# Batch 1's convolution on 64-by-32 tiles in a causal-convolution and low-rank-mixer kernel, with two-group slots up to group 9 and batches 3 to 7 loaded and convolved a slot later

## Chip, cores, metric

One core of one Trainium2 chip. The metric is the device time of one execution in microseconds (us); with one core it is that core's time. The kernel before takes 325.07 us (median; 324.9 to 325.2). Within a trace the span is a little shorter (323.2 us for a run of 324.98 us), and all instants below are microseconds from the start of the span.

## The reference, cut to what matters

```python
# x: (8, 4224, 192); weight: (8 heads, 7 taps); U: (4224, 32); V: (32, 4224); w_ch1: (192, 768); w_ch2: (768, 192)
w = softmax(weight, axis=-1)
# causal convolution along the sequence, one set of 7 taps per head of 24 channels
y = einsum('hk,bskhg->bshg', w, windows_of_7(x_padded)).reshape(B, S, D)
# mixer: a low-rank product along the sequence, then two products along the channels
h = (y.transpose(0, 2, 1) @ U) @ V
u = y + h.transpose(0, 2, 1)
out = u + relu(u @ w_ch1) @ w_ch2
```

## The kernel before

TensorE does everything that is a product. The 264 tiles of 128 sequence rows make 33 groups of 8; each batch is 33 tiles, so a batch ends inside a group. A group goes through these helpers, whose names stand in the schedule (line numbers in profiles are those of the kernel before; those of the changed kernel are 6 higher from the convolution on):

- `conv32` (L339) or `conv` (L369): a batch's convolution as products with band matrices. `conv32` works on eight 64-by-32 tiles of the array, but needs `xb_sb`, a copy of x shifted by whole blocks and half blocks. `conv` works on four 64-by-64 tiles straight from `x_sb`. Evictions from PSUM go to `y_sb`.
- `t` and `s` (L402, L428): the product with U, for a whole batch. `h` (L457) is the product with V, and VectorE adds it to y into `u_sb` (L479).
- `transp` (L498): SyncE transposes `u_sb` by DMA into `uT`.
- `w1` (L554): 36 matmuls of the first product from `uT`, with 12 relu evictions; `w2` (L583): 12 matmuls of the second product for two tiles, plus an addition on VectorE and the output DMA on SyncE.

The shifted copy is made by GpSimd in six steps; its buffer is single:

```python
xbs = ctx.enter_context(tc.tile_pool(name="xbs", bufs=1))
...
def x_shift(b):
    xbt[b] = xbs.tile([P, NB1, D], BF16, name="xb_sb")
    ...                       # same(): L293 and L295, ahead(): L305, all nc.gpsimd.tensor_copy
    return [same(0, m), same(m, NB0, (NB0, NB1)),
            ahead(0, 0, m), ahead(0, m, NB0), ahead(1, 0, m), ahead(1, m, NB1)]
```

The same GpSimd queue issues the loads of x (four per batch), each held back until a named first or second product has run (`x_load(b, q, after)`). The order of everything is written out in slots: first the first products of some groups, then second products in pieces of two tiles, and other work hung on piece numbers (`c2:0:3` is three heads of batch 2's convolution from head 0 on, with letters for the evicting engines, A for ScalarE and D for VectorE; `d1` is batch 1's convolution by `conv`; `l2:2` a load of batch 2; `x3:4` four steps of batch 3's shifted copy; `h8` the residual of group 8 followed by its transpose; in the change, `X` is GpSimd's part of batch 1's copy and `w0:0` one of SyncE's transfers for it):

```python
SLOTS = [
    ([0], [], {}),
    ([1], [0], {0: ["h0"], 1: ["h3", "l2:2"], 2: ["l2:3"]}),
    ([2], [1], {0: ["d1", "h1"], 1: ["t1"], 3: ["s1"], 4: ["h4", "x2:6"]}),
    ([3], [2], {1: ["h5"], 3: ["h6"]}),
    ([4, 5], [3, 4, 5], {0: ["h7"], 2: ["c2:0:3:AAD"], 3: ["c2:3:3:AAD"],
        4: ["c2:6:2:A", "x3:4"], 6: ["t2"], 8: ["s2"], 9: ["h8"], 11: ["h9"]}),
]
nh = 10                       # next group to get its h and its transpose
for k in range(5, 14):        # slots [6, 7, 8], [9, 10, 11], ... [30, 31, 32]
    ...                       # h of groups nh, nh+1, nh+2 at pieces 5, 8 and 11
LOADS = {2: [(1, 5), (1, 5)], 3: [(4, 1), (4, 4), (5, 1), (5, 4)]}
for b in range(4, B):         # batch b's loads wait for first products of groups 3b-6 and 3b-5
    g = 3 * b - 6
    LOADS[b] = [(g, 0), (g, 3), (g + 1, 0), (g + 1, 3)]
```

The transpose of group 12 is issued in the last pieces of the slot of groups 6 to 8, and group 12 is wanted only after the whole slot of groups 9 to 11.

## Time and profile before

| | kernel before |
|---|---|
| time, us | 325.07 |
| span of the profiled run, us | 323.2 |
| TensorE busy | 317.6 us, 98% |
| granted TensorE clock | 0.9 or more in all 40 slices, mean 1.00 |
| median landing of a quarter of x, of a transpose | 6.9 us, 3.5 us |
| `h` and transpose ahead of the slot that uses them | one group more than needed |

The chain of waits in order of time, for the slot of groups 9 to 11: three groups' first products, then the first part of a convolution.

```profile
109.46 11.76 PE ps L554 x108
121.22 0.47 PE ps L339 x11
```

The view of the tile `uT`, SyncE's transposes alone, first all of them and then those issued between 130 and 140 us (counts, durations of the issue in ns, then the time from issue to landing, the arrival of the last data, in us):

```profile
L498 SPq DMA_TRANSPOSE uT<-u_sb x31: 1274/1437/2920, 27.1 to 291.6; - x31
DMA to landing us min/median/max: 3.2/3.5/8.3
```
```profile
L498 SPq DMA_TRANSPOSE uT<-u_sb x3: 1274/1537/2271, 132.0 to 139.0; - x3
DMA to landing us min/median/max: 4.2/4.9/7.9
```

The reader should not stop at the median. As long as loads of x go on, one transpose in each slot takes about twice as long: the one issued at 67.3 us took 8.3 us to land, those at 110.7, 139.0 and 167.6 us took 6.7, 7.9 and 7.1. Each of the last three is issued within 1 us of a load of x (GpSimd issues them at 111.0, 138.5 and 166.7). In the kernel before this costs nothing, because the group is not wanted for another whole slot (issued at 139.0, wanted at 165.57).

### The profile page before, as it was taken

How to read it: one execution, taken by the hardware profiler on the slowest of the kernel's cores; microseconds unless marked ns; L12 is line 12 of the kernel's file. 1: busy time of each engine (PE TensorE's matmuls, PEld its weight loads, DVE VectorE, ACT ScalarE, POOL GpSimd, SP SyncE). 2: the span in 40 equal slices, each digit the busy share in tenths (PEclk: the TensorE clock that was granted, in tenths of full speed). 3: DMA queues.
4: the chain of work that ended last, by engine and by line, in shares of the span. 5: the costliest groups of instructions: out<-in, count | busy, mean ns of one | idle time of the engine just before them, and what ended most of it. 6: DMA issues, size and time to landing. Idle time of an engine off the chain costs nothing.

```text
span 323.2 us, 9583 instructions
## 1 busy us (share of the span) xinstructions
PE 317.6 (98%) x3996; PEld 223.7 (69%) x3996; DVE 268.6 (83%) x551; ACT 170.0 (53%) x344; POOL 142.7 (44%) x111
## 2 busy tenths in 40 slices
PE   8999999999999999999999999999999999999995
PEld 3747676478677647866864884687797497487495
DVE  6769989987977986997898699789888897896863
ACT  1766724860874397088239609824903902912910
POOL 8764179728957983992897497000000000000000
PEclk9999999999999999999999999999999999999999
DMA  9999993999998999599499957138268059048035
GB/s 106 192 191 183 206 209 100 196 192 257 208 135 200 246 142 190 166 189 209 130 237 192 181 149 194 52 105 231 61 178 262 3 150 275 18 121 271 2 121 173
DMA packets 122906, 53.51 MB, mean 166 GB/s; under 512 B 87760, under 2 KB 122832, under 8 KB 122864
## 3 DMA queue, kind: packets, MB, share of 16 engines
q1 hardware_dynamic: 84528, 38.08, 45.4%
q0 software_dynamic: 38192, 14.73, 39.2%
q8 instruction: 31, 0.51, 0.7%
q10 hardware_dynamic: 144, 0.10, 0.1%
q14 instruction: 11, 0.09, 0.1%
HBM read 29.49 MB, written 25.95 MB: 172 GB/s over the span
## 4 chain that ended last, share of the span: by engine, by line
PE 92%; ACT 3%; DMA 2%; DVE 1%; issue 0%; POOL 0%; POOLq 0%
PE ps L583 42%; PE ps L554 39%; PE ps L339 3%; PE ps L457 3%; DMA x_sb<-in_x_dram 2%; PE ps L402 2%; ACT rl_sb L568 2%; PE ps L369 1%; ACT y_sb L256 1%; PE ps L509 1%; DVE u_sb L479 1%; DVE rl_sb L570 1%; PE ps L524 0%; PE ps L428 0%; POOL x_sb L79 0%
## 5 line engine op out<-in xcount | busy, mean ns | idle before, releaser
L568 ACT ACTIVATE rl_sb<-ps 128x512 bf16<-128x512 f32 x233 | 124.3, 604 | 108.0 <-PE ps L554 96.0
L583 PE MATMUL ps<-W_sb,rl_sb 128*128 128x192 bf16 x1584 | 141.2, 246 | 0.2
L583 PEld LDWEIGHTS <-rl_sb 128*128 128x128 bf16 x1584 | 128.3, 98 | 11.8 <-issue 11.5
L554 PE MATMUL ps<-uT,W_sb 64*128 64x512 bf16 x1188 | 131.7, 376 | 0.0
L570 DVE TENSOR_SCALAR rl_sb<-ps 128x512 bf16<-128x512 f32 x163 | 105.3, 688 | 15.7 <-PE ps L554 15.4
L554 PEld LDWEIGHTS <-W_sb 64*128 64x128 bf16 x1188 | 66.9, 94 | 60.4 <-issue 3.9
L592 DVE TENSOR_TENSOR out_sb<-ps,u_sb 128x384 f32<-128x384 f32 (+1 forms) x133 | 70.4, 551 | 25.5 <-PE ps L583 25.0
L305 POOL COPY xb_sb<-x_sb 32x3072 bf16<-32x3072 bf16 (+1 forms) x24 | 67.4, 2824 | 0.5
L479 DVE TENSOR_TENSOR u_sb<-y_sb,ps 128x192 bf16<-128x192 bf16 (+1 forms) x168 | 66.3, 461 | 0.0
L293 POOL COPY xb_sb<-x_sb 128x3072 bf16<-128x3072 bf16 x12 | 32.7, 2742 | 42.1 <-PE ps L339 32.2
L256 ACT ACTIVATE y_sb<-ps 128x384 bf16<-128x384 f32 (+4 forms) x90 | 38.3, 520 | 9.7 <-PE ps L339 7.4
L79 POOL DMA_DIRECT2D x_sb<-in_x_dram x32 | 27.0, 848 | 9.6 <-PE ps L457 3.8
L258 DVE CAST y_sb<-ps 128x408 bf16<-128x408 f32 (+4 forms) x36 | 19.1, 578 | 1.3 <-PE ps L369 1.0
L457 PE MATMUL ps<-tt_sb,V_sb 32*128 32x192 bf16 x264 | 12.4, 246 | 0.1
L339 PE MATMUL ps<-x_sb,band 64*32 64x384 bf16 x192 | 12.1, 333 | 0.0
L339 PE MATMUL ps<-xb_sb,band 64*32 64x384 bf16 x192 | 12.1, 332 | 0.0
L457 PEld LDWEIGHTS <-V_sb 32*128 32x128 bf16 x264 | 4.7, 92 | 7.3 <-issue 7.3
L416 ACT ACTIVATE tt_hi<-ps 128x192 bf16<-128x192 f32 x8 | 2.6, 330 | 11.9 <-PE ps L402 11.9
L369 PE MATMUL ps<-x_sb,band 64*64 64x240 bf16 (+3 forms) x192 | 8.0, 276 | 0.2 <-DMA x_sb<-in_x_dram 0.2
L339 PEld LDWEIGHTS <-band 64*32 64x32 bf16 x384 | 4.5, 89 | 5.2 <-issue 2.4
L153 PE MATMUL ps<-zz 128*128 128x512 f32 (+1 forms) x10 | 6.7, 816 | 1.1 <-DVE zz L143 1.1
L369 PEld LDWEIGHTS <-band 64*64 64x64 bf16 x192 | 6.0, 106 | 2.1 <-issue 1.4
(65 smaller groups left out, 71.3 us busy)
## 6 DMA issues: line engine op xcount, KB each, us to landing
out_dram<-out_sb SPq DMA_DIRECT2D x131, 192.0 KB, 2.7
x_sb<-in_x_dram POOLq DMA_DIRECT2D x14, 384.0 KB, 6.9
x_sb<-in_x_dram POOLq DMA_DIRECT2D x7, 432.0 KB, 6.7
x_sb<-in_x_dram POOLq DMA_DIRECT2D x7, 408.0 KB, 8.0
x_sb<-in_x_dram POOLq DMA_DIRECT2D x1, 504.0 KB, 7.3
uT<-u_sb SPq DMA_TRANSPOSE x31, 3.5
x_sb<-in_x_dram POOLq DMA_DIRECT2D x1, 480.0 KB, 5.6
W_sb<-in_moe_w_ch_dram POOLq DMA_DIRECT2D x2, 192.0 KB, 7.8
```

The costliest lines, as they stand in the source:

```text
L79: return nc.gpsimd.dma_start(out=xt[b][HB * r : HB * r + HB, s0:s1, :], in_=x[b, blk * HB : (blk + s1 - s0) * HB, :].rearrange("(j p) d -> ...
L256: nc.scalar.activation(out=out, in_=in_, func=ACT.Copy)
L293: nc.gpsimd.tensor_copy(out=xbt[b][:, s0:s1, :], in_=xt[b][:, s0 + 1 : s1 + 1, :])
L305: nc.gpsimd.tensor_copy(out=xbt[b][q, s0:s1, :], in_=xt[b][q, s0:s1, :])
L339: nc.tensor.matmul(out=pp[r][QB * cg : QB * cg + QB, 0 : nk[r] * GS], lhsT=w[hr], rhs=t[hr, st : st + 2 * nk[r] - 1 : 2, hs], start=True, ...
L457: nc.tensor.matmul(out=banks[pr][:, a * D : (a + 1) * D], lhsT=V_sb[32 * q : 32 * q + 32, (j // 8) * 2 + j % 2, :], rhs=ttb[b][32 * q : 32 ...
L479: nc.vector.tensor_tensor(out=u_group(g)[:, i : i + n, :, hf, :], in0=yt[b][:, run[0] : run[0] + n, :].rearrange("p n (c k) -> p n c k", c=3),
L554: last = nc.tensor.matmul(out=pps[m][hf][:], lhsT=W1_sb[HB * hf : HB * hf + HB, c, m * P : (m + 1) * P], rhs=uTt[g][HB * hf : HB * hf + HB ...
L568: nc.scalar.activation(out=rl[:, m, hf, :], in_=pp[hf][:], func=ACT.Relu)
L570: nc.vector.tensor_scalar_max(out=rl[:, m, hf, :], in0=pp[hf][:], scalar1=0.0)
L583: last = nc.tensor.matmul(out=cps[:, a * D : (a + 1) * D], lhsT=rlt[g][:, m, hf, (i + a) * P : (i + a + 1) * P], rhs=W2_sb[:, m, :], start ...
L592: nc.vector.tensor_tensor(out=o[:, 0:n, :].rearrange("p n (c k) -> p n c k", c=3), in0=cps[:, 0 : n * D].rearrange("p (n c k) -> p n c k", ...
```

## The change

Its intent: batch 1's convolution costs 3.24 us on 64-by-64 tiles and its evictions hold the end for 5.6 us. The change puts it on 64-by-32 tiles in three pieces between second products. The shifted copy it needs is made half by GpSimd (three steps) and half by three SyncE transfers. To make room, the early slots take two groups instead of one or three, the loads, copies and convolutions of batches 3 to 7 come a slot later, and `h` is made one group less far ahead; below, this distance is called the lookahead.

```diff
+    def x_ahead(b, r, n):
+        ...
+        nc.sync.dma_start(out=xbt[b][q, s0:s1, :], in_=xt[b][q, s0:s1, :])
     SLOTS = [
-        ([0], [], {}),
-        ([1], [0], {0: ["h0"], 1: ["h3", "l2:2"], 2: ["l2:3"]}),
-        ([2], [1], {0: ["d1", "h1"], 1: ["t1"], 3: ["s1"], 4: ["h4", "x2:6"]}),
-        ([3], [2], {1: ["h5"], 3: ["h6"]}),
-        ([4, 5], [3, 4, 5], { ... "c2" at 2, 3, 4, "x3:4" at 4, "t2" at 6, "s2" at 8, "h8" at 9, "h9" at 11 }),
+        ([0], [], {0: ["X", "w0:0", "w1:0"]}),
+        ([1], [0], {0: ["h0"], 1: ["h3"], 2: ["w0:1"]}),
+        ([2], [1], {0: ["h1"], 2: ["c1:0:3:AAD"], 3: ["c1:3:3:AAD"], 4: ["c1:6:2:AD", "x2:6"]}),
+        ([3], [2, 3], {0: ["t1"], 1: ["s1"], 2: ["h4"], 5: ["h5"]}),
+        ([4, 5], [4, 5], {0: ["h6"], 3: ["h7"], 5: ["c2:0:2:A"], 6: ["c2:2:3:AAD"], 7: ["c2:5:3:AAD"]}),
+        ([6, 7], [6, 7], {0: ["x3:4", "t2"], 1: ["s2"], 2: ["h8"], 5: ["h9"]}),
+        ([8, 9], [8, 9], {0: ["h10"], 2: ["c3:0:2:A"], 3: ["c3:2:3:AAD"], 4: ["c3:5:3:AAD", "x4:4"],
+            5: ["h11"], 6: ["t3"], 7: ["s3"], 8: ["h12"]}),
     ]
-    nh = 10
-    for k in range(5, 14):            # slots [6, 7, 8], [9, 10, 11], ...
+    nh = 13
+    for g in range(10, NG, 3):        # slots [10, 11, 12], [13, 14, 15], ...
 ...
-    LOADS = {2: [(1, 5), (1, 5)], 3: [(4, 1), (4, 4), (5, 1), (5, 4)]}
-    for b in range(4, B):
-        g = 3 * b - 6
-        LOADS[b] = [(g, 0), (g, 3), (g + 1, 0), (g + 1, 3)]
+    LOADS = {b: [(g, 0), (g, 3), (g + 1, 0), (g + 1, 3)]
+             for b, g in enumerate([6, 8] + list(range(10, NG, 3)), 3) if b < B}
 ...
+        if what == "X":               # GpSimd's half of batch 1's copy, then all four loads of batch 2
+            ...
```

More of the change, by code (lines that the diff above doesn't have):

```diff
@@ L317, in x_shift @@
         ]
+    def x_ahead(b, r, n):
+        q = slice(HB * r + QB, HB * r + HB)
+        s0, s1 = ((0, NB0 // 2), (NB0 // 2, (NB0, NB1)[r]))[n]
+        nc.sync.dma_start(out=xbt[b][q, s0:s1, :], in_=xt[b][q, s0:s1, :])
     steps = []
@@ L619 @@
     SLOTS = [
-        ([0], [], {}),
-        ([1], [0], {0: ["h0"], 1: ["h3", "l2:2"], 2: ["l2:3"]}),
-        ([2], [1], {0: ["d1", "h1"], 1: ["t1"], 3: ["s1"], 4: ["h4", "x2:6"]}),
-        ([3], [2], {1: ["h5"], 3: ["h6"]}),
+        ([0], [], {0: ["X", "w0:0", "w1:0"]}),
+        ([1], [0], {0: ["h0"], 1: ["h3"], 2: ["w0:1"]}),
+        (
+            [2],
+            [1],
+            {
+                0: ["h1"],
+                2: ["c1:0:3:AAD"],
+                3: ["c1:3:3:AAD"],
+                4: ["c1:6:2:AD", "x2:6"],
+            },
+        ),
+        ([3], [2, 3], {0: ["t1"], 1: ["s1"], 2: ["h4"], 5: ["h5"]}),
         (
             [4, 5],
-            [3, 4, 5],
+            [4, 5],
             {
-                0: ["h7"],
-                2: ["c2:0:3:AAD"],
-                3: ["c2:3:3:AAD"],
-                4: ["c2:6:2:A", "x3:4"],
-                6: ["t2"],
-                8: ["s2"],
-                9: ["h8"],
-                11: ["h9"],
+                0: ["h6"],
+                3: ["h7"],
+                5: ["c2:0:2:A"],
+                6: ["c2:2:3:AAD"],
+                7: ["c2:5:3:AAD"],
+            },
+        ),
+        ([6, 7], [6, 7], {0: ["x3:4", "t2"], 1: ["s2"], 2: ["h8"], 5: ["h9"]}),
+        (
+            [8, 9],
+            [8, 9],
+            {
+                0: ["h10"],
+                2: ["c3:0:2:A"],
+                3: ["c3:2:3:AAD"],
+                4: ["c3:5:3:AAD", "x4:4"],
+                5: ["h11"],
+                6: ["t3"],
+                7: ["s3"],
+                8: ["h12"],
             },
@@ L638 @@
     ]
-    nh = 10
-    for k in range(5, 14):
-        gs = list(range(3 * k - 9, 3 * k - 6))
-        hs = [f"h{g}" for g in range(nh, min(nh + 3, NG))] + [None] * 3
+    nh = 13
+    for g in range(10, NG, 3):
+        gs = list(range(g, min(g + 3, NG)))
+        hs = [f"h{n}" for n in range(nh, min(nh + 3, NG))] + [None] * 3
         nh = min(nh + 3, NG)
-        if k == 5:
-            at = {
-                2: ["c3:0:3:AAD"],
-                3: ["c3:3:3:AAD"],
-                4: ["c3:6:2:A", "x4:4"],
-                5: [hs[0]],
-                6: ["t3"],
-                8: ["s3", hs[1]],
-                11: [hs[2]],
-            }
-        elif k < 10:
-            b = k - 2
+        b = (g + 2) // 3
+        if b < B:
             at = {
@@ L668 @@
     assert nh == NG
-    LOADS = {2: [(1, 5), (1, 5)], 3: [(4, 1), (4, 4), (5, 1), (5, 4)]}
-    for b in range(4, B):
-        g = 3 * b - 6
-        LOADS[b] = [(g, 0), (g, 3), (g + 1, 0), (g + 1, 3)]
+    LOADS = {
+        b: [(g, 0), (g, 3), (g + 1, 0), (g + 1, 3)]
+        for b, g in enumerate([6, 8] + list(range(10, NG, 3)), 3)
+        if b < B
+    }
     late = piece_tiles(2)
@@ L768, in do @@
             return
-        if what[0] == "d":
-            for h in range(H):
-                last = conv(int(what[1:]), h, 1, [0, 1], "AA" if h == 2 else "AD")
-            held(transp(3), last)
+        if what == "X":
+            st = x_shift(1)
+            for n in (0, 1, 5):
+                st[n]()
+            x_tile(2)
+            x_zero(2, nc.gpsimd)
+            for q in (0, 2, 1, 3):
+                x_part(2, *XP[q])
             return
-        if what[0] == "l":
-            b, q = (int(v) for v in what[1:].split(":"))
-            x_load(b, q, done_w2[-1])
+        if what[0] == "w":
+            x_ahead(1, *(int(v) for v in what[1:].split(":")))
             return
@@ L786, in do @@
             h_group(n)
-            if n > 1 and n != 3:
+            if n > 1:
                 transp(n)
@@ L804 @@
                 do("h2")
-        while steps and gs1 != [3]:
+        while steps:
             steps.pop(0)()
```

## The prediction

> **What bounds the kernel now.** I read the busy shares first, then the chain of waits in order of time, then the timelines of TensorE and GpSimd, then a table of engine work by stretch. The page's first part:
>
> ```profile
> PE 317.6 (98%) x3996; PEld 223.7 (69%) x3996; DVE 268.6 (83%) x551; ACT 170.0 (53%) x344; POOL 142.7 (44%) x111
> ```
>
> TensorE is in use almost without a break, so a gain must come from less matmul work, or from matmuls that stand waiting while they count as busy. The chain in order of time shows where that is so. In the stretch with batch 1's convolution it reads (start, length, what):
>
> ```profile
> 33.83 2.09 PE ps L554 x18
> 35.92 2.54 ACT rl_sb L568 x5
> 38.47 3.10 ACT y_sb L256 x8
> 41.56 0.04 issue
> 41.60 1.15 PE ps L583 x12
> ```
>
> For 5.6 us ScalarE's evictions carry the end, not the matmuls. Elsewhere (lines 554 and 583, first and second product of the mixer) the chain is TensorE 92% of the span. TensorE's timeline has batch 1's convolution as one piece, here above those of a later batch on the chain, which run in three pieces between second products:
>
> ```profile
> 37.75 3.24 PE L369 MATMUL ps<-x_sb,band 64*64 64x384 bf16 x64
> ```
> ```profile
> 95.08 0.64 PE ps L339 x19
> 96.81 0.71 PE ps L339 x17
> 98.62 0.47 PE ps L339 x11
> ```
>
> The same 64 matmuls cost 3.24 us on 64-by-64 tiles and 0.64 + 0.71 + 0.47 = 1.82 us on 64-by-32 tiles. The price of the latter is a shifted copy of x, made by GpSimd. One round of it:
>
> ```profile
> 99.23 5.42 POOL L293 COPY xb_sb<-x_sb 128x3072 bf16<-128x3072 bf16 x2 [6.18 <-PE ps L339]
> 104.72 0.50 POOL L295 COPY xb_sb<-x_sb 32x384 bf16<-32x384 bf16 x1
> 105.26 5.43 POOL L305 COPY xb_sb<-x_sb 32x3072 bf16<-32x3072 bf16 x2
> 110.75 0.17 POOL L74 MEMSET x_sb<- 64x96 uint32 x1
> 111.00 0.82 POOL L79 DMA_DIRECT2D x_sb<-in_x_dram  x1
> 111.86 2.74 POOL L305 COPY xb_sb<-x_sb 32x3072 bf16<-32x3072 bf16 x1
> 114.55 0.81 POOL L79 DMA_DIRECT2D x_sb<-in_x_dram  x1
> 115.35 3.08 POOL L305 COPY xb_sb<-x_sb 32x3456 bf16<-32x3456 bf16 x1
> 118.36 1.72 POOL L79 DMA_DIRECT2D x_sb<-in_x_dram  x2
> 126.35 2.74 POOL L293 COPY xb_sb<-x_sb 128x3072 bf16<-128x3072 bf16 x1 [6.27 <-PE ps L339]
> ```
>
> The reader should see a loop: the buffer of the shifted copy is single, so a round starts when the previous convolution's last matmul has read it (the release by line 339), takes 99.23 to 118.36 = 19.1 us, and the next convolution starts at 121.22 in the chain. So there are 2.9 us of slack in a 28 us slot, and GpSimd, at 44% of the whole, is 75% busy there.
>
> [...] the copies of 3072 elements last 2.74 us whether beside VectorE work or not, so I count no contention. [...] Here a quarter of x takes 6.9 us from issue to landing at the median.
>
> **The change part by part.** The matmul and issue counts stay, except three added transfers on SyncE, four added GpSimd copies (two of 2.74, 0.50 and 3.08 us = 9.1 us) and one more slot (15 for 14).
>
> *Start, to the end of the second products of group 5.* Nothing moves before 29 us. Batch 1's x has landed by about 29 us (the GpSimd DMA queue is full without a gap until then), so its copies run about 27 to 36.5 us; convolution 1 comes after the first products of group 2 (about 37.9), h1 and two second products, so near 40.3: covered. Its evictions (10 on ScalarE at 0.52, 6 on VectorE at 0.55) now lie among the second products. VectorE comes into that slot 1.4 us behind (its three out_sb adds end at 35.2), and following it through h1, out_sb and y_sb adds gives the start of group 3's first products at 44.85 us. The old kernel starts them at 47.12 us but has by then done t1, s1 and h4 (0.85 + 0.17 + 0.34 = 1.36), so 45.76 like for like: 0.9 gained, from the 1.4 us that the tiles save. Going on at 4.0 per first product, 1.04 per pair of second products[...], 1.82 for convolution 2, I come to 78.8 us for the start of group 6's first products; the old kernel is there at 81.09 less t2, s2, h8, h9 (1.72) = 79.4. **Gain 0.6 us.**
>
> *Slot of groups 6 and 7.* t2 and s2 are one second product apart, where there were two. s2 needs a ScalarE copy that queues behind 14 relus (14 x 0.604 = 8.5 us against 8 us of matmuls), then a VectorE subtraction: some 0.4 us of wait. h8 comes 6 second products before its use: adds 2.07, transpose issue 1.4 and landing, 6.5 to 7 us in all, against 6.6: 0.2 of wait. **Loss 0.6.**
>
> *Slot of groups 8 and 9.* Call T the 78.8. The loads of batch 3 are held to T+1.1, 3.0, 5.0 and 7.0; the last two should land near T+10 and T+12.5. The copies: to T+15.5 and 16.1, two more to 21.5, an issue 22.6, copy 25.4, issue 26.2, copy 29.3. Convolution 3 stands at T+18.8 (next slot) + 7.9 + 0.35 + 2.1 = T+29.2. Just met: **loss 0.3**.
>
> *Slot of groups 10 to 12.* This is the step that decides. From the last matmul of convolution 3 to the first of convolution 4 TensorE has 4 second products (4.3), h11, h12 (0.7), t3, s3 (1.0) and three first products (11.9): 17.9 us. GpSimd needs 19.1 us, so at least 1.3 us of wait. Moreover the last two loads of batch 4 are issued only after convolution 3's copies, as in every round; they took 7.3 to 8.5 us (from 118.36, queue packets end at 125.6), convolution 3 only 4.3, so the second copy may wait for its load: about 1.2 more. **Loss 1.3 to 2.5, taken 1.9.** Later rounds have 23.6 us from convolution to convolution and fit, as now.
>
> [...] Sum: -0.6 + 0.6 + 0.3 + 1.9 + 0.2 = +2.4; 325.07 + 2.4 = 327.5, rounded down to 327.2 because waits overlap: a wait at s2 or at a first product gives GpSimd time.
>
> **The rivals.** (1) The change simply gains 1 to 4 us: two-group slots relieve VectorE, and the 3.0 us that the old kernel loses between 20.5 and 81 us beyond its plain matmul times come back. For it: the ScalarE pieces on the chain. Against: VectorE's work there hardly changes (it is busy 54 of 60.6 us in the table by stretch). It would give 321 to 324. (2) GpSimd becomes the bound over two or three rounds, with convolution 3 late by 2 us as well[...]: 330 to 332. (3) The three SyncE transfers block the transposes queued behind them: the first waits for a GpSimd copy near 30 us, but the next transpose is not needed until 44.8 us, so hidden: 0.
>
> **Range and chances.** The terms are uncertain by about 1 us each early and 1.5 us at convolutions 3 and 4: range 323.0 to 331.0. Over 2% faster is under 318.6: it would need all the early loss back and no wait at all, 0.04. Over 2% slower is above 331.6: rival 2 in full, 0.08. Within 2%: 0.88.
>
> **What would show it.** Convolution 1 at about 1.9 us of matmuls in three pieces; group 6's first products near 78.8; in the slot of groups 10 to 12 a TensorE gap of 1 to 3 us ahead of convolution 4, with GpSimd's copy as releaser; GpSimd at 9 tenths over some 100 to 135 us; the steady slots at 28 us as before. Wrong if convolution 4 has no wait, if convolution 3 waits over 1.5 us, or if the first 80 us shrink by over 2.

(The sum came to +2.4 us, 327.5, taken as 327.2. One of its terms is 0.2 us for the extra slot. Measured on the chain of the kernel before, the 12 matmuls of a pair of second products take 0.99 us after matmuls on tiles of the same 128-by-128 form, as at 45.85 us, and 1.10 to 1.15 after those on other tiles, as at 51.53 and 55.27; why is not shown, and the 0.2 is the author's estimate.)

## The result, and the profile after

The changed kernel takes 345.0 us (median of six; 338.93 to 349.08) where the kernel before takes 325.07 (324.9 to 325.2): a ratio of 1.052, with a 95% interval of 1.045 to 1.060. A ratio is the mean time of one kernel's fast runs over that of the other's of the same rounds, so it is not quite the ratio of the medians. The changed kernel scatters by 3%, and three of its six runs are marked slow, being over 1.5% above its fastest. Its three fast runs have a mean of 342.0 us and a mean clock of 0.984. Its profiled run is the slowest one (349.08 us, span 347.3, mean clock 0.966). I therefore rely on those waits in it that come back in profiles of fast runs: all four do, above all in the experiment e15 below.

From the changed kernel's page, busy shares, the granted clock in 40 slices, the chain by engine, and three rows of the costliest groups:

```profile
PE 326.6 (94%) x3996; PEld 225.0 (65%) x3996; DVE 268.9 (77%) x550; ACT 171.4 (49%) x345; POOL 151.7 (44%) x115
...
PEclk9999999999998998799699969999999999999999
...
PE 72%; DMA 11%; POOL 10%; DVE 4%; ACT 1%; issue 1%; POOLq 0%; DVEq 0%
...
L560 PE MATMUL ps<-uT,W_sb 64*128 64x512 bf16 x1188 | 137.8, 389 | 6.9 <-DMA uT<-u_sb 6.9
...
L345 PE MATMUL ps<-xb_sb,band 64*32 64x384 bf16 x224 | 15.6, 347 | 8.1 <-POOL xb_sb L305 8.1
```

Where TensorE led the chain for 92% of the span it now leads for 72%; transfers and GpSimd have 21%. TensorE waits 6.9 us for transposes and 8.1 us for GpSimd's copies, 15.0 us in all, and it runs below full clock in some slices (6 to 8 tenths in five of the 40). The chain of waits in order of time says where:

```profile
106.22 3.09 POOL xb_sb L305
109.35 0.88 PE ps L345 x11
110.23 2.03 PE ps L589 x12
...
134.84 3.09 POOL xb_sb L305
137.97 0.88 PE ps L345 x11
...
156.55 2.48 PE ps L560 x22
159.04 8.64 DMA uT<-u_sb
167.72 7.02 PE ps L560 x29
...
192.15 9.65 DMA uT<-u_sb
201.84 7.02 PE ps L560 x35
...
225.12 11.76 PE ps L560 x108
```

Four places. Convolutions 3 (109.35) and 4 (137.97) go on when GpSimd's last copy ends; TensorE, after one matmul of each, had been idle for 3.20 and 4.94 us. In the slots of groups 13 to 15 and 16 to 18, the third group's first products wait for a transpose that takes 8.64 and 9.65 us; TensorE had stopped at 164.6, so 3.1 us idle in the first. Both transposes were issued next to a load of x (transposes at 159.04 and 192.15, loads at 157.64, 161.19 and 192.09). At 225.12 three groups run in one piece of 11.76 us, as in the kernel before. After each wait the matmuls are slow: 12 matmuls of L589 take 2.03 us instead of 1.10, and the piece of first products after each transpose takes 7.02 us instead of some 3.95. The table by stretch (window, length, busy time of TensorE, weight load, VectorE, ScalarE, GpSimd, then granted clock, DMA share and GB/s) has, of the changed kernel, the slots of groups 10 to 12, 13 to 15 and 19 to 21, and the stretch after the first of the two transposes:

```profile
120.66:156.55 35.89, 30.95 (x378) 23.61 (x379) 24.35 (x53) 16.62 (x34) 28.98 (x17) 0.90 0.81 140
156.55:190.92 34.37, 31.23 (x376) 20.90 (x375) 24.18 (x49) 16.83 (x34) 20.58 (x13) 0.90 0.93 156
...
225.10:253.10 28.00, 28.00 (x378) 18.80 (x379) 23.97 (x52) 16.51 (x34) 6.11 (x3) 1.00 0.45 127
...
167.70:174.70 7.00, 6.98 (x44) 2.42 (x46) 2.61 (x4) 3.45 (x6) 0.00 (x0) 0.57 1.42 182
```

A three-group slot with a convolution takes 28.0 us when nothing waits, a two-group one some 20.1 by an estimate (28.0 less 3.92 for a group's first products and 4.0 for its second). So the slot of groups 8 and 9 (95.60 to 120.66) lost some 5.0 us, that of 10 to 12 lost 7.9, the next two 6.3 and 6.2; the early part gained 1.5 (group 6's first products start at 77.9 us instead of 79.4 like for like). The sum is 23.9 of the 24.1 us between the two spans. It can be split in another way: the 15.0 us of waits, and the lost share of clock in the stretches after them. By the same view the latter is 3.55 us at 0.58 after convolution 3's wait, 4.80 at 0.50 after convolution 4's, 7.00 at 0.57 and 7.10 at 0.57: 1.5 + 2.4 + 3.0 + 3.1 = 10.0 us. That is the slow profiled run. In the fast runs a mean clock of 0.984 over 342 us allows at most 5.5 us.

In each of the four stretches the granted clock stands at 0.50 first, in the same view with finer windows, and then goes back to 1.00: for 3.0 us from 109.35 on, 5.0 from 137.97, 6.0 from 167.7 and 6.0 from 201.84. The gaps of TensorE before them are 3.20, 4.94, 3.14 and 2.97 us. The length of a gap does not by itself say what follows. After one of 1.81 us in e14 (to 70.29) two pieces of 12 second products took 1.59 and 1.78 us instead of 1.15, in a slice (67 to 76 us) that its page gives 7 tenths of the clock, and after one of 2.15 in e1 (to 138.86) 24 took 3.61 instead of 2.09. After one of 2.94 in e5 (to 137.76) 24 took 2.09.

### The profile page after: what moved, and what is told of

The parts are those of the page before. It is cut to its first block, busy times and chain, and to the rows that moved or that the text cites. A ratio compares the mean times of both kernels' runs of the same rounds, so it can differ in the third digit from the quotient of the medians.

```text
span 347.3 us, 9599 instructions
## 1 busy us (share of the span) xinstructions
PE 326.6 (94%) x3996; PEld 225.0 (65%) x3996; DVE 268.9 (77%) x550; ACT 171.4 (49%) x345; POOL 151.7 (44%) x115
## 4 chain that ended last, share of the span: by engine, by line
PE 72%; DMA 11%; POOL 10%; DVE 4%; ACT 1%; issue 1%; POOLq 0%; DVEq 0%
PE ps L589 33%; PE ps L560 29%; DMA uT<-u_sb 7%; POOL xb_sb L305 6%; DMA x_sb<-in_x_dram 4%; PE ps L345 4%; DVE u_sb L485 3%; PE ps L463 2%; PE ps L408 2%; POOL xb_sb L293 2%; POOL x_sb L79 1%; DVE out_sb L598 1%; ACT rl_sb L574 1%; PE ps L375 1%; PE ps L515 1%
## 5 line engine op out<-in xcount | busy, mean ns | idle before, releaser
L589 PE MATMUL ps<-W_sb,rl_sb 128*128 128x192 bf16 x1584 | 144.2, 250 | 0.1
L560 PE MATMUL ps<-uT,W_sb 64*128 64x512 bf16 x1188 | 137.8, 389 | 6.9 <-DMA uT<-u_sb 6.9
L589 PEld LDWEIGHTS <-rl_sb 128*128 128x128 bf16 x1584 | 130.4, 99 | 12.4 <-issue 11.9
L305 POOL COPY xb_sb<-x_sb 32x3072 bf16<-32x3072 bf16 (+1 forms) x25 | 70.5, 2834 | 0.6
L293 POOL COPY xb_sb<-x_sb 128x3072 bf16<-128x3072 bf16 x14 | 38.2, 2742 | 58.3 <-PE ps L345 31.9
L256 ACT ACTIVATE y_sb<-ps 128x408 bf16<-128x408 f32 (+4 forms) x91 | 38.8, 512 | 27.5 <-PE ps L345 25.1
L345 PE MATMUL ps<-xb_sb,band 64*32 64x384 bf16 x224 | 15.6, 347 | 8.1 <-POOL xb_sb L305 8.1
L345 PE MATMUL ps<-x_sb,band 64*32 64x384 bf16 x224 | 14.9, 349 | 0.0
L408 PE MATMUL ps<-y_sb,U_sb 128*32 128x192 bf16 x258 | 7.4, 248 | 0.0
L408 PEld LDWEIGHTS <-U_sb 128*32 128x32 bf16 x258 | 5.4, 96 | 1.9 <-issue 1.6
```

What stands on the lines that cost most here:

```text
L256: nc.scalar.activation(out=out, in_=in_, func=ACT.Copy)
L293: nc.gpsimd.tensor_copy(out=xbt[b][:, s0:s1, :], in_=xt[b][:, s0 + 1 : s1 + 1, :])
L305: nc.gpsimd.tensor_copy(out=xbt[b][q, s0:s1, :], in_=xt[b][q, s0:s1, :])
L345: nc.tensor.matmul(out=pp[r][QB * cg : QB * cg + QB, 0 : nk[r] * GS], lhsT=w[hr], rhs=t[hr, st : st + 2 * nk[r] - 1 : 2, hs], start=True, ...
L560: last = nc.tensor.matmul(out=pps[m][hf][:], lhsT=W1_sb[HB * hf : HB * hf + HB, c, m * P : (m + 1) * P], rhs=uTt[g][HB * hf : HB * hf + HB ...
L589: last = nc.tensor.matmul(out=cps[:, a * D : (a + 1) * D], lhsT=rlt[g][:, m, hf, (i + a) * P : (i + a + 1) * P], rhs=W2_sb[:, m, :], start ...
```

## The experiments

Fifteen kernels ran, each against the kernel before on the same chip, whose median stayed between 325.0 and 325.2 us in all rounds. All gave correct results. Medians are of all runs of a kernel, ratios of its fast runs alone.

### e1: the lookahead of one group given back

Theory: h15 and h18 come too late because `h` is made one group less far ahead. Rival: the transposes are late whatever the schedule.

```diff
-                8: ["h12"],
+                8: ["h12", "h13"],
-    nh = 13
+    nh = 14
```

> The changed kernel with h13 emitted one slot earlier, so that every later group's residual adds and transpose come one group earlier, as in the kernel before; nothing else. Theory (three causes that add): the two waits for uT ahead of the first products of groups 15 and 18 (3 us idle each, then matmuls at half clock, 6.3 and 6.2 us over a plain slot) vanish, the two waits at convolutions 3 and 4 stay: 345 less 12.5 = about 332 us. Rival (the added transfers and copies load the DMA queues, and the transposes are late wherever they stand): the waits only move, and the time stays above 340.

Measured: 336.85 us (336.3 to 337.5), ratio 1.036. In its chain in time, the two slots that lost 6 us each have their three groups' first products in one piece again; the second of them:

```profile
184.74 11.76 PE ps L560 x108
```

So 8 of the 20 us between the medians, or 5 of 17 us between the fast runs, come from the lookahead. That is short of the 12.5 us that those slots lost in the slow profile, and of the theory's 332 us. A transpose beside a load still takes 9.54 us in e1, but it is now group 16's, which is not wanted for another slot. TensorE still waits 5.0 us for GpSimd's copies at convolutions 3 and 4, as the theory says.

### e2 and e3: loads of batches 3 and 4 a slot earlier, without and with e1

Theory: convolutions 3 and 4 wait because their loads are held too long. If so, earlier loads remove those waits, and e3 has nothing left to wait for.

```diff
+    LOADS[3] = [(4, 1), (4, 4), (5, 1), (5, 4)]
+    LOADS[4] = [(6, 0), (6, 3), (7, 0), (7, 3)]     # and x3:6 right after c2, x4:6 right after c3
```

> The changed kernel with batches 3 and 4 loaded one slot earlier and copied right after the convolution before (all six copies ahead of the next batch's loads); lookahead as in the changed kernel. Theory: the waits of TensorE for GpSimd's copies at convolutions 3 and 4 (4.9 and 7.9 us over plain slots) vanish, those for uT stay: 345 less 12.8 = about 332 us. Rival (GpSimd is simply too slow for one round per slot once batch 1 is added): the wait at convolution 4 stays at 1.3 us or more and with it half of the loss, 338 or above.

> Both edits together. Theory: the losses are separate and add, so no wait over 1 us is left and the gain of batch 1's tiles shows: 321 to 323 us, under the kernel before (325.1), and the spread of the changed kernel (339 to 349) goes with the waits. Rival (batch 1's added copies and transfers cost by themselves): 326 or above.

Measured: e2 341.22 us (339.0 to 349.4), ratio 1.047; e3 337.32 us (336.3 to 347.95), ratio 1.036; one run of each is slow. Both theories miss. In e2 the waits for GpSimd shrank to 0.8 us as expected, but 10.5 us of waits for transposes took their place. The chain of e2:

```profile
74.32 13.80 DMA uT<-u_sb
```

This transpose, group 7's, was issued at 74.32 us beside four loads of x that GpSimd issues back to back from 71.47 on; the shortest transpose in these traces takes 3.2 us. The ones issued at 54.14 and 147.68 us took 6.00 and 8.52 us and were waited for, 1.9 and 3.1 us. In e3 the same transpose took 14.85 us. The gain of e3 over e2 and its lack of gain over e1 show that the losses do not add. A load moved away from one transpose meets another.

### e4: TensorE kept busy through the four waits

Theory: the half clock (0.50 after gaps of 2.97 to 4.94 us, in the changed kernel's profile) is a loss of its own. I put dummy matmuls into a spare PSUM bank ahead of each of the four waits (18, 22, 14, 14), so that only the clock differs.

```diff
+            if g in (15, 18):
+                warm(14)
+                2: ["W18", "c3:0:2:A"],             # and W22 ahead of convolution 4
```

> The changed kernel with matmuls that nobody reads put ahead of the four waits (18 and 22 of 128 by 512 ahead of convolutions 3 and 4, 14 ahead of groups 15 and 18), so that TensorE works while it would stand idle. All waits are kept. Theory (after each idle gap of 3 us or more the granted clock falls to about half, and this costs 1.4, 2.3, 3.1 and 3.2 us): the clock stays at 1.0 and 8 to 10 us come back, though not the idle time: 335 to 337 us. Rival (the clock figure is only a mark of idleness and the slow matmuls wait for their data): no gain or a loss of up to 4 us, 344 to 349.

Measured: 343.42 us (342.7 to 345.5), ratio 1.057, clock 1.00; a miss. In the chain of e4, convolution 4, the end of its slot, and the third group's first products after the first of the two transposes:

```profile
140.39 0.54 PE ps L345 x10
...
156.63 8.02 PE ps L560 x72
...
167.79 3.99 PE ps L560 x36
```

The clock is whole (1.00), and the work after each wait is shorter. From convolution 4 to the end of its slot it takes 16.24 us (140.39 to 156.63) instead of 18.58; from convolution 3 (111.91 in e4) to the end of its slot (121.85) 9.94 instead of 11.31. The two later slots took 31.46 and 31.25 us instead of 34.37 and 34.18, since 36 first products needed 4.0 us instead of 7.02. So the half clock cost 1.4, 2.3, 2.9 and 2.9 us, near the sum of 10 us above. But the time did not come back. Convolution 4 started 2.4 us later in e4 (140.39), because a load of batch 4 landed only 12.14 us after its issue. The dummy matmuls also ran on for about 1 us after convolution 3's copies (to 111.9 us, the copies to 110.9) and after each transpose had landed (at 166.57, first products at 167.79). Against the changed kernel's median the gain is 1.6 us, inside its scatter; against its fast runs there is none.

### e5: loads of batches 6 and 7 held until the transposes have landed

Theory: the loads make the transposes slow. Rival: the short lookahead alone makes the wait.

```diff
+    LOADS[6] = [(15, 0), (15, 0), (15, 3), (15, 3)]
+    LOADS[7] = [(18, 0), (18, 0), (18, 3), (18, 3)]     # and all six copy steps at once for batches 5 and 6
```

> The changed kernel with its lookahead unchanged; only the loads of batches 6 and 7 are held until the third first product of their slots (groups 15 and 18), by when the transposes of these groups should have landed, and the copies of batches 5 and 6 run without loads between them. Collision theory (a transpose issued among x loads takes 8 to 14 us[...]; alone it takes 3.2 to 4): the waits for uT at groups 15 and 18 go although each group's h still comes as late as in the changed kernel, about 12 us back: 331 to 335, and the waits at convolutions 3 and 4 stay. Rival (the lookahead is too short whatever the loads do): the waits stay, 340 or more.

Measured: 338.74 us (337.9 to 339.6), ratio 1.042. In the chain of e5 the waits at groups 15 and 18 are gone although the lookahead is as short as in the changed kernel; but the chain now runs through the loads, which are slow in a burst:

```profile
154.01 10.63 PE ps L560 x96
...
165.76 12.94 DMA x_sb<-in_x_dram
...
195.96 14.91 DMA x_sb<-in_x_dram
```

The theory holds for these two waits, though not for its 331 to 335 us: without loads beside them, the two transposes take 3.58 and 3.51 us and land in time. The price is a load of 13 to 15 us where the median is 7, and a burst at 193.5 us that catches the transposes of groups 19 and 20 (7.64 and 6.81 us; TensorE waits 2.0 and 0.8 us). The waits at convolutions 3 and 4 stay, 3.57 and 2.94 us.

### e6: the kernel before, with one group less of lookahead

The opposite test: only the lookahead of the kernel before is shortened.

```diff
-                9: ["h8"],
-                11: ["h9"],
+                11: ["h8"],
-    nh = 10
+    nh = 9
```

> The kernel before with one group less of lookahead (h8 alone in the slot of groups 4 and 5, then three per slot as before, from h9): tiles, loads and slots are those of before. Theory: the third first product of each slot that also loads x (groups 8, 11, 14, 17) waits for its transpose and then runs at half clock for 3 us: 3 to 6 us each, so 337 to 349. Rival (only the changed kernel's DMA order makes transposes late): at most 328.

Measured: 338.25 us (332.5 to 340.4), ratio 1.030, within the theory's 337 to 349 by its median. Two of its four runs are marked slow; the fast ones took 332.5 and 337.2 us, so they are late too. Its chain (of the slowest run) has the changed kernel's wait in three slots:

```profile
110.47 8.80 DMA uT<-u_sb
...
119.32 5.75 PE ps L554 x36
...
143.57 8.72 DMA uT<-u_sb
...
152.34 5.75 PE ps L554 x36
```

The third is at 176.25, of 9.52 us. After the first two, 36 first products take 5.75 us instead of some 3.95. These transposes stand where one took 6.7 to 7.9 us in the kernel before at no cost. One group of lookahead is what hides them: with it the late one belongs to the next slot's first group, without it to the third group of the slot that has just begun.

### e7 to e12: can the change's idea be had without its waits?

e7 keeps batch 1 on small tiles, gives back the lookahead and the three-group slots from group 6 on, and has SyncE shift batch 2 as well. e9 moves the convolutions forward by one or two pieces. e11 puts batch 2's SyncE transfers ahead in SyncE's queue. e8, e10 and e12 are the same three with batch 1 on 64-by-64 tiles.

```diff
-        ([4, 5], [4, 5], {...}), ([6, 7], ...), ([8, 9], ...)
+        ([4, 5], [4, 5], {... c2 at 3, 4, 5, t2 at 6, s2 at 7, h8 at 8}),      # e7
+        ([6, 7, 8], [6, 7, 8], {0: h9, c3 at 4, 5, 6, "h10" at 5, "h11" at 8, "h12" at 11 ...}),
+    LOADS = {3: [(4, 1), (4, 4), (5, 1), (5, 4)], 4...: groups 3b-6 and 3b-5, as before}
```

> A version meant to keep the gain: batch 1 on 64-by-32 tiles as in the change, slots and lookahead of the kernel before from group 6 on, loads where they were before, batch 2 shifted by SyncE and GpSimd as well (8.2 us less on GpSimd), convolutions 3 and later two second products later in their slots. Theory: GpSimd then finishes batch 2 near 61 us as before, no copy and no transpose is late, and the 1.5 us gained before group 6 stay: 323 to 324. Rival (SyncE's transfers or the tighter early slots cost what the tiles save): 325 or more.

Measured: 330.08 us (329.1 to 331.0), ratio 1.015: 15 us better than the changed kernel (12 between fast runs), still 5 worse than before, as the rival had it. It waits 1.9 us for the transpose of group 4, 1.6 us for GpSimd at convolution 4.

> The same with batch 1 back on 64-by-64 tiles (no shift of batch 1, its convolution in the same three places). Theory: slower than e7 by the time saved on the tiles, 1.2 us (3.0 against 1.8 us of matmuls), if nothing else is late: 324.5 to 325.5. Rival (the tiles save nothing on the chain because evictions bound that slot): equal to e7 within 0.4 us.

Measured: 336.74 us (335.7 to 337.5), ratio 1.035, a flawed comparison. Without batch 1's copies in front of them, GpSimd issued batch 2's loads at 25.5 us, some 12 us earlier than e7, and the transpose of group 2 was caught among them and took 11.24 us. TensorE's timeline in e8:

```profile
38.47 6.44 PE L560 MATMUL ps<-uT,W_sb 64*128 64x512 bf16 x36 [4.61 <-DMA uT<-u_sb]
```

An unplanned second case, early in the kernel, of loads in a burst that make a transpose late.

> e7 with the early convolutions moved forward: convolution 1 one second product earlier and t1 ahead of group 3's first products (so h4's transpose comes 1.9 us earlier), convolution 2 two pieces earlier, h6 and h7 no longer next to each other, convolution 3 one piece earlier. Theory (e7 loses 1.9 us at uT of group 4, about 2 us where VectorE must make room for h6 and h7, and 4 us at convolution 4, whose copies start late because convolution 3's did): these go, and 322.5 to 324.5 is left, just under the kernel before (325.1). Rival (GpSimd and the x loads have no slack once batch 1 is added, so convolution 4 waits wherever the others stand): 327 or more.

Measured: 330.86 us (328.6 to 332.3), ratio 1.016. That is the rival's number without its mechanism: no wait is left at convolutions 3 and 4, and from 86 us on the slots with a convolution take 28.9 and then 28.2 us. One long wait is left, at convolution 2, for SyncE's transfers, which run beside the loads of batch 3. From the chain of e9:

```profile
63.83 8.78 DMA xb_sb<-x_sb
```

In the changed kernel, which issues them before the loads of batch 2 (at 31.3 to 36.1 us, the loads from 37.85 on), such transfers took 3.0 to 3.2 us.

> e9 with batch 1 on 64-by-64 tiles, without its shifted copy and transfers, batch 2's loads held to the end of group 2's first products, which is when they are issued in e9. Theory: the tiles save 1.2 us of matmuls that lie on the chain, so this is 0.8 to 1.6 us slower than e9. Rival (the slot is bound by evictions): equal to e9 within 0.4 us.

Measured: 329.72 us (328.9 to 330.6), ratio 1.013, so no slower than e9: in this arrangement small tiles for batch 1 bring nothing measurable. The product with U for batch 1 ends at 45.94 us in e9 and at 46.72 in e10, 0.8 us for the small tiles, but both finish group 3's first products at 50.7 to 50.9.

> e9 with SyncE's x transfers moved ahead in its queue: those of batch 2 ahead of h5's transpose and three output writes, the last of batch 1 ahead of h3's transpose. Theory (e9's only long wait is convolution 2 waiting from 68.7 to 72.6 us for the transfers of batch 2, which were issued behind the output writes[...]; about 4 us and 2 us at half clock): 324.5 to 326. Rival (the transfers take 8 us wherever they stand): 329 or more.

> e10 (batch 1 on 64-by-64 tiles) with the transfers of batch 2 moved in the same way: 323.5 to 325 by the first theory, 328 or more by the rival. Against e11 it gives the worth of batch 1's tiles where nothing is late: 1.2 us for the tiles if the matmuls count, nothing or less if evictions and SyncE's transfers take it back; e9 and e10 suggest the latter.

Measured: 332.76 us (331.9 to 333.5) and 332.91 us (331.3 to 334.9), ratios 1.023 and 1.024; both miss. The earlier SyncE transfers landed in 2.8 to 3.8 us and freed convolution 2, so the rival's mechanism fails as well. But the transpose of group 5, now behind them, met the loads of batch 3: in e12 it was issued at 61.39, beside a load at 61.50, and took 8.15 us, where in e10 it was issued at 59.20 and took 3.45.

### e13 to e15: the change's parts one at a time

What was open: which part of the change brings the loss, the small tiles of batch 1 (with its copies), the early two-group slots, or the later loads with the short lookahead. e13 takes the early two-group slots alone (batch 1 on 64-by-64 tiles, loads and lookahead as before, no SyncE transfers). e14 takes batch 1's tiles and copies alone, in the slots of the kernel before, with the loads of batch 2 behind batch 1's copies as in the change and the others as before. e15 takes the change's slots, loads and lookahead and leaves batch 1 and the loads of batch 2 as before.

```diff
 # e14: slots of the kernel before, except
-        ([0], [], {}),
+        ([0], [], {0: ["X", "w0:0", "w1:0"]}),
-        ([2], [1], {0: ["d1", "h1"], ...
+        ([2], [1], {0: ["h1"], 1: ["c1:0:8:AD"], ...
 # e15: slots of the change, except
-                2: ["c1:0:3:AAD"], 3: ["c1:3:3:AAD"], 4: ["c1:6:2:AD", "x2:6"],
+                2: ["d1:0:3"], 3: ["d1:3:3"], 4: ["d1:6:2", "x2:6"],     # d1: 64-by-64 tiles
+    LOADS[2] = [(1, 5), (1, 5)]
```

> Only the early two-group slots of the change: batch 1 on 64-by-64 tiles, the loads of batch 2 when they were in the kernel before, GpSimd alone for batch 2's copies, no transfers by SyncE, three-group slots with the old lookahead from group 6 on (as e12 otherwise). Theory (what made e7 to e12 late is batch 1's 9 us on GpSimd and the 8.5 us later loads of batch 2 that follow from it): nothing is late, and some 1 us gained early stays: 323.5 to 325. Rival (the early two-group slots are themselves too tight for the transposes): 328 or more.

Measured: 325.77 us (325.45 to 327.4), ratio 1.003 (1.001 to 1.005), clock 1.00, a little above the theory's 325: the two-group slots cost next to nothing and gain nothing.

> Only batch 1's tiles: its shift by GpSimd and SyncE and its convolution on 64-by-32 tiles, in the slots and with the lookahead and load positions of the kernel before. Theory: batch 2's x is loaded 8.5 us later and its copies end near 69 instead of 60 us, while convolution 2 stands at 65: a wait of 4 us and half clock after it, then loads and copies of batches 3 and 4 about 5 us late in turn: 330 to 336. Rival (the whole loss of the change comes from its slots and its shorter lookahead): 323.5 to 325, a gain of about 1 us.

Measured: 339.17 us (337.4 to 340.6), ratio 1.044, more than the theory's 330 to 336. Here is what the prediction had called covered. GpSimd's timeline, first of the kernel before, then of e14:

```profile
29.29 2.48 POOL L79 DMA_DIRECT2D x_sb<-in_x_dram  x3 [3.83 <-PE ps L457]
...
45.35 2.74 POOL L293 COPY xb_sb<-x_sb 128x3072 bf16<-128x3072 bf16 x1 [1.41 <-DMA x_sb<-in_x_dram]
```
```profile
37.81 3.36 POOL L79 DMA_DIRECT2D x_sb<-in_x_dram  x4
...
55.65 2.74 POOL L293 COPY xb_sb<-x_sb 128x3072 bf16<-128x3072 bf16 x1 [3.57 <-DMA x_sb<-in_x_dram]
```

Batch 1's copies do fit beside TensorE's work, but GpSimd is also the engine that issues the loads, and in its queue they stand behind the copies. (No run puts them between the copies.) Batch 2's loads start 8.5 us later, in one burst, and the second copy of batch 2 starts 10.3 us later. The loop of load, copy, convolution is late from then on: convolution 2 waits 1.8 us, and convolution 3 waits in TensorE's timeline of e14:

```profile
105.09 0.49 PE L345 MATMUL ps<-xb_sb,band 64*32 64x408 bf16 x1 [5.07 <-POOL xb_sb L305]
```

> Only the change's slots, lookahead and later loads from batch 3 on; batch 1 on 64-by-64 tiles and the loads of batch 2 as in the kernel before. Theory: the waits at convolutions 3 and 4 and at the transposes of groups 15 and 18 come from the slots alone, so all of them are here too: 340 to 347. Rival (they need batch 1's added work on GpSimd and the DMA queues): below 333.

Measured: 345.61 us (342.6 to 349.7), ratio 1.061, as much as the whole change and as the theory had it. TensorE's waits in e15, a fast run (waiting line and releaser: us in all, times, longest):

```profile
PE ps L345 <- POOL xb_sb L305: 8.2, 2, 4.8
PE ps L560 <- DMA uT<-u_sb: 7.5, 5, 3.0
```
These are the changed kernel's 8.1 and 6.9 us, at the same places; on the chain the transposes of groups 15 and 18 take 8.44 and 9.22 us. The comparison also shows what the small tiles are worth in the change's own slots. Group 6's first products on the chain, in the changed kernel and in e15:

```profile
77.89 4.68 PE ps L560 x42
```
```profile
79.25 6.63 PE ps L560 x60
```

In e15 the first products of group 0 were already 0.16 us later (24.99 instead of 24.83 us), so the tiles bring some 1.2 us by here, in one profile of each (e1 and e5, with small tiles, begin these products at 78.5 and 77.9); the later waits cover it.

As for the losses, the two parts lose 4.4% and 6.1% by themselves and 5.2% together. I read this so: the change's later slots are the room that batch 1's copies need, and the late loads and short lookahead that come with them are a loss of their own.

No version beat the kernel before; e13 comes nearest, 0.3% slower.

## Why the prediction was wrong

The prediction, 327.2 us with a range of 323 to 331, was wrong: 345.0. One of its own signs of being wrong came true, a wait of over 1.5 us at convolution 3 (3.20 us). Point by point:

1. **The early part: right in kind, small in size.** Convolution 1 ran in three pieces at the predicted cost; group 6's first products were predicted at 78.8 us and began at 77.9. The gain was 1.5 us, not 0.6; some 1.2 of it are the tiles' (e15), near the 1.4 that the prediction gave them. The 0.6 us expected to be lost in the slot of groups 6 and 7 did not show.
2. **"Later rounds have 23.6 us from convolution to convolution and fit, as now": this step failed.** It asked only about GpSimd. The slots of groups 13 to 15 and 16 to 18 lost 12.5 us of the 24 in the slow profile, and e1 gives 5 of 17 us for fast runs, at a place that no rival names. The prediction's 6.5 to 7 us for h8's adds, issue and landing leave some 3.5 us for the landing, the median, and it looked at the lookahead for group 8 only. It did not ask which transposes make up the maximum of 8.3 us, nor that they lie beside the loads of x. In the change the transposes of groups 15 and 18 took 8.64 and 9.65 us and had 5.5 and 6.7 us until TensorE wanted them; in the kernel before, those of the same groups took 7.94 and 7.14 us and had 26.6 and 26.0. e1 (lookahead back: waits gone), e5 (loads moved: waits gone) and e6 (lookahead of the kernel before shortened: waits appear) show both conditions, a load beside the transpose and one group less of lookahead.
3. **"This is the step that decides", convolution 4: right mechanism, mis-sized term.** It gave 1.3 to 2.5 us, of which 1.2 for loads; the slot lost 7.9. TensorE's own way from the end of convolution 3's last matmul (114.74) to convolution 4's first (132.69) took 17.95 us, as predicted (17.9), and GpSimd's round 19.85 (19.1, which less 17.9 is 1.2 and not 1.3). But the round began 3.3 us after that last matmul, at 118.07: batch 4's last two loads, issued from 109.2 us on, landed 8.71 and 11.28 us later, and the second copy waited another 0.57 us within the round. The term had 1.2 us for it. 3.3 + 19.85 - 17.95 gives 5.2, of which TensorE stood idle for 4.94. Most of the rest was clock. The gap varies: it is 2.15 us in the fast profile of e1 and 4.83 in that of e15.
4. **Convolution 3, "just met": mis-sized.** Loss 5.0 us instead of 0.3. The first copies began 12.05 us after T, the start of group 6's first products, where the prediction has 10, so loads were about 2 us late; TensorE came 1.2 us earlier than planned. Together these make the wait of 3.20 us. The half clock added 1.5 us.
5. **The clock was left out of the sum.** By the table by stretch it is some 10 us in the profiled run, a slow one, and e4 confirms each part (1.4, 2.3, 2.9 and 2.9 us); in the changed kernel's fast runs it is at most 5.5 us.
6. **Rival 2** (GpSimd becomes the bound for two rounds, 330 to 332) named the right engine for half of the loss. **Rival 3** was right for the changed kernel, where the SyncE transfers cost nothing seen. In e9 such transfers for batch 2 took 7.9 to 8.8 us among loads, and in e11 and e12 a transpose queued behind them came late.
7. **"Covered" copies of batch 1.** True of TensorE's time, but e14 shows that they push batch 2's loads back by 8.5 us, because GpSimd both copies and issues. (The last of batch 1's own loads landed at 30.9 us in the kernel before, not by "about 29"; it cost nothing.)

Not settled: why a transpose and loads beside each other take two to four times as long (3.2 to 14.85 us for a transpose, the longest in e3; 5.2 to 15.5 for a load, the longest on the chain of e14). No run separates the possible causes. The share of the DMA engines' time that is in use does not tell the two cases apart: in the kernel before, the transpose at 195.93 us, after the last load of x, took 3.25 us at a DMA share of 1.08, and that at 110.65, beside a load, 6.70 at 1.11. No run gives the shifted copy a second buffer, so what its single one costs is not shown. Nor is it shown that the changed kernel's scatter of 3% comes from the landing of loads, though that of batch 4's last load differs (10.4 us in e5, 11.3 in the changed kernel, 12.1 in e4).

## What to carry to other kernels

Before removing a group of lookahead, find the slowest transfer that it hides, not the median (here 8.3 us, not 3.5), and what runs beside it. Work put on an engine that also issues loads can cost the delay of those loads, even when its own time is free (8.5 us in e14). The four waits of 3.0 to 4.9 us on TensorE cost 1.4 to 2.9 us more by the clock here (against e4), so a forecast with such a wait should ask for that term too, unless another engine's loop sets the end anyway, as in e4.
